# Second attention: heads 0 to 15 of three tiles first, and four projections moved into the steps

## Chip, cores, metric

One core of one Trainium2 chip. The metric is the time of one execution of the whole program on the device, in microseconds, as the median of several runs. Where a part of the program is meant, its time is read from the trace.

## The reference

Four layers run one after the other on a residual stream `x` of 2048 rows and 576 columns: attention (A), gMLP (B), A, B. The change touches the second A alone.

```python
def _A_ref(x, wqkv, wo):            # H = 32 heads of Dh = 18; W = 8 keys at distance 0, 2, .. 14 back
    qkv = (x @ wqkv)...             # q, k, v by head
    logits = einsum('bhsd,bhswd->bhsw', q, kg) * Dh ** -0.5     # masked where the key lies before row 0
    o = einsum('bhsw,bhswd->bhsd', softmax(logits), vg)
    return o... @ wo
x = x + _A_ref(_layernorm(x), A_wqkv, A_wo)
x = x + _B_ref(_layernorm(x), ...)
x = x + _A_ref(_layernorm(x), A_wqkv, A_wo)
x = x + _B_ref(_layernorm(x), ...)
```

## The kernel before

The attention cuts the rows into 19 tiles of 112 queries with a halo of 16 keys. A *step* `s` is one tile and one half of the heads: tile `s // 2`, heads 0 to 15 where `s` is even, 16 to 31 where it is odd. The main loop runs 38 steps. In each, PE makes the next step's logits (`L_mm`), ScalarE their exponentials (`EXP`), and PE multiplies the previous probabilities by v (`PV`); then come other pieces from a table: projections of q and k for later columns (`PG`), of v (`VW`), output projections of finished rows (`WO`), layer norms.

```python
def L_mm(s):
    t, hf = divmod(s, 2)
    L_tiles[s] = [self.H_tile("L_ps") for _ in range(2)]     # two tiles of two PSUM banks, a ring of 2
    ...                                                      # 16 matmuls, reading QK
def PV(s):
    ...                                                      # 16 matmuls into O_ps, then on VectorE:
    nc.vector.reciprocal(...)
    nc.vector.tensor_tensor(out=o_t[:nq, 288 * hf:288 * (hf + 1)]..., op=ALU.mult)
    if hf == 1:                                              # both halves there: transpose by DMA, from SP
        nc.sync.dma_start_transpose(out=oT[:, :, c0:c0 + nq], in_=o_t[:nq, :])
def WO(i, hh):                                               # row tile i of 128 rows: two tiles of oT
    for c in range(5):
        nc.tensor.matmul(pw[:, 0:288], lhsT=oT[:, c, r0:r0 + P], rhs=wo_sb[...], ...)
```

A projection lands in a staging tile. When the last one of a staging tile is there, eight DMA moves carry it, head by head, to the places in QK where the logits read it; they go to the queues of POOL and SP in turn.

```python
for dst, src in moves:
    dma_rr[0] += 1
    self.dma(dst, src, eng=queues[dma_rr[0] % len(queues)])
...
def XO(i):                                                   # residual rows for two row tiles, 576 KB, from SP
    self.dma(xo[:], x_prev[i * P:(i + 2) * P, :]..., eng=nc.sync)
def XST(i): self.dma(self.xres[li][...], tails[i]["x"][:])   # store, from SP
def LN_T(i): self.ln_T(...)                                  # transpose of the normed rows, from SP
```

The table, and the loop:

```python
PG_END = 14
pre, pgs = pgs[:6], pgs[6:]          # 18 projections; six ahead of the loop
for k_, (d, qk, cc) in enumerate(pgs):
    at(1 + k_ if li == 0 else (k_ * PG_END) // len(pgs), PG, d, qk, cc, True)
for i in range(NS):
    t = -(-(i + 1) * P // QT) - 1    # the last tile that row tile i needs
    s = 2 * t + (6 if li == 0 and t < 10 else 5 if t < NT - 5 else 4 if t < NT - 3 else 3)
    at(s - 5, XO, i); at(s, WO, i, 0); at(s + 1, WO, i, 1) ...
at(PG_END + 2, alloc_win2b)          # weights of the next layer, six loads from POOL, steps 16 to 26
...
for s in range(NST):
    if s + 1 < NST:
        L_mm(s + 1)
        EXP(s + 1)
    PV(s)
    for f, a in table.pop(s, []):
        f(*a)
```

SP issues in program order: output transposes, moves, loads, stores and the transposes of the normed rows all stand in one line.

The softmax here doesn't subtract the row's maximum and nothing guards it: scores larger than these inputs give would overflow.

## Time and profile before

| | value |
|---|---|
| time, median of 3 runs | 1190.21 us (1190.11 to 1192.29) |
| profiled span | 1190.8 us |
| start of the second attention (its first projection) | 601.25 us |
| from there to the start of the layer's last PV, called *layer time* below | 115.68 us |
| from there to the end | 473.89 us |

The last three rows add up to the span. The prediction below shows the page and the stretches of the layer.

### The profile page before, as it was taken

To read this page: it belongs to the slowest core of one execution; us is meant where nothing else is said; L and a number is where in the kernel's file an instruction comes from. 1 tells how busy PE (TensorE), PEld (TensorE's weight loads), DVE (VectorE), ACT (ScalarE), POOL (GpSimd) and SP (SyncE) were. 2 spreads that over 40 slices of the span, in tenths; PEclk is the share of its full clock that TensorE was granted. 3 is DMA by queue.
4 is the path that set the end of the run, shared out by engine and by line. 5 is a ranking of instruction groups with operands and counts; after the bars stand their busy time and mean duration, and the time that the engine had idled before them with its cause. 6 is when DMAs were issued, how large, how long until landed. Compare 5 with 4: busy or idle time off the path is not lost.

```text
span 1190.8 us, 20761 instructions
## 1 busy us (share of the span) xinstructions
PE 1180.2 (99%) x8554; PEld 620.6 (52%) x8554; DVE 547.4 (46%) x1206; ACT 376.6 (32%) x593; POOL 281.5 (24%) x383
## 2 busy tenths in 40 slices
PE   8999999999999999999999999999999999999998
PEld 5567544444444444457755775444444444444677
DVE  8688587333233233245556786753233233233311
ACT  5578677210110110202156786760110110111000
POOL 4768685000000000001153877530000000000000
PEclk9999999999999999999999999999999999999999
DMA  8989992000000000049645999900000000000332
GB/s 195 200 163 199 181 224 65 23 4 9 12 12 12 12 1 11 12 139 291 169 98 117 203 227 196 202 14 9 12 12 1 12 12 12 12 1 28 125 105 73
DMA packets 178104, 101.21 MB, mean 85 GB/s; under 512 B 134336, under 2 KB 159360, under 8 KB 178009
## 3 DMA queue, kind: packets, MB, share of 16 engines
q1 hardware_dynamic: 165144, 78.13, 30.6%
q0 software_dynamic: 6512, 16.00, 5.4%
q10 hardware_dynamic: 6352, 5.75, 1.6%
q8 instruction: 67, 1.10, 0.4%
q14 instruction: 29, 0.23, 0.1%
HBM read 42.39 MB, written 16.53 MB: 49 GB/s over the span
## 4 chain that ended last, share of the span: by engine, by line
PE 94%; DMA 3%; POOL 1%; ACT 0%; issue 0%; SPq 0%; DVE 0%; ACTq 0%; DVEq 0%
PE pg L887 42%; PE pz L869 12%; PE po L941 12%; PE pz L791 11%; PE pp L402 5%; PE pw L494 3%; PE O_ps L457 3%; PE pv L379 3%; PE L_ps L437 2%; DMA oT<-o_t 2%; PE pzs L791 1%; DMA QK<-win2a 1%; POOL QK L77 1%; DMA wqk_sb<-in_A_wqkv_dram 1%; ACT P_sb L446 0%
## 5 line engine op out<-in xcount | busy, mean ns | idle before, releaser
L887 PE MATMUL pg<-Wq,Z 128*128 128x512 bf16 x2304 | 502.8, 379 | 0.0
L887 PEld LDWEIGHTS <-Z 128*128 128x128 bf16 x2304 | 225.3, 98 | 272.0
L891 DVE TENSOR_TENSOR g_tmp<-pg,ln_xn 128x512 f32<-128x512 f32 x144 | 99.6, 692 | 429.2 <-PE pg L887 429.2
L881 ACT ACTIVATE z1T<-pz 128x1024 bf16<-128x1024 f32 x72 | 73.7, 1024 | 513.8 <-PE pz L869 513.6
L77 POOL DMA_DIRECT2D wout<-in_B_w_out_dram x4 | 4.3, 1064 | 604.6 <-PE pg L887 604.6
L941 PE MATMUL po<-wout,Z 128*128 128x288 bf16 x1152 | 141.4, 286 | 0.0
L446 ACT ACTIVATE P_sb<-L_ps 128x896 bf16<-128x896 f32 (+1 forms) x152 | 126.7, 887 | 41.2 <-PE L_ps L437 40.6
L869 PE MATMUL pz<-xnT,w 128*128 128x512 bf16 (+1 forms) x640 | 136.0, 380 | 0.0
L941 PEld LDWEIGHTS <-Z 128*128 128x128 bf16 x1152 | 112.7, 98 | 28.8
L791 PEld LDWEIGHTS <-xnT 128*128 128x128 bf16 (+1 forms) x800 | 66.2, 97 | 81.0 <-issue 23.7
L791 PE MATMUL pz<-win2a,xnT 128*128 128x512 bf16 x384 | 104.8, 380 | 0.0
L892 DVE TENSOR_TENSOR Z<-g_tmp,z1T 128x512 bf16<-128x512 f32 x144 | 99.6, 692 | 9.7
L869 PEld LDWEIGHTS <-w 128*128 128x128 bf16 (+1 forms) x640 | 51.1, 97 | 80.0 <-issue 27.1
L402 PE MATMUL pp<-xnT,wqk_sb 128*128 128x512 bf16 x360 | 83.8, 382 | 0.5 <-DMA wqk_sb<-in_A_wqkv_dram 0.5
L805 ACT ACTIVATE zp<-pz 128x1024 bf16<-128x1024 f32 x64 | 65.5, 1024 | 36.6 <-PE pz L791 32.8
L951 DVE TENSOR_TENSOR x_new<-po,xo 128x288 f32<-128x288 f32 (+1 forms) x64 | 28.8, 455 | 87.6 <-PE po L941 83.5
L791 PE MATMUL pz<-win2b,xnT 128*128 128x512 bf16 (+1 forms) x256 | 65.7, 380 | 0.0
L807 DVE CUSTOM_DVE_ANT_0 Z<-zp 128x1536 bf16<-128x1536 bf16 x32 | 56.6, 1769 | 13.1 <-ACT zp L805 13.0
L77 POOL DMA_DIRECT2D QK<-stg x81 | 50.7, 631 | 36.3 <-DVE stg L371 21.0
L379 PE MATMUL pv<-wv_sb,xnT 128*128 128x288 bf16 (+1 forms) x380 | 55.8, 285 | 0.0
L242 POOL TENSOR_SCALAR ln_xn<-x_new,ln_mv,ln_rstd 128x576 bf16<-128x576 f32 x23 | 52.8, 2294 | 2.0
L402 PEld LDWEIGHTS <-wqk_sb 128*128 128x128 bf16 x360 | 33.2, 98 | 37.2 <-DMA wqk_sb<-in_A_wqkv_dram 1.0
(114 smaller groups left out, 916.9 us busy)
## 6 DMA issues: line engine op xcount, KB each, us to landing
xres<-x_new SPq DMA_DIRECT2D x48, 288.0 KB
xo<-xres SPq DMA_DIRECT2D x32, 288.0 KB
wout<-in_B_w_out_dram POOLq DMA_DIRECT2D x4, 1296.0 KB, 8.5
xo<-xres SPq DMA_DIRECT2D x8, 576.0 KB
w<-in_B_w_in_dram SPq DMA_DIRECT2D x16, 256.0 KB
QK<-stg POOLq DMA_DIRECT2D x53, 72.0 KB, 4.4
QK<-stg SPq DMA_DIRECT2D x41, 72.0 KB
xo<-in_A_x_dram SPq DMA_DIRECT2D x8, 288.0 KB
```

The lines of the kernel that those rows point to most:

```text
L77: return eng.dma_start(out=out, in_=in_)
L379: nc.tensor.matmul(pv[:nk, 0:288], lhsT=self.xnT[:, c, QT * t:QT * t + nk], rhs=wv_sb[:, c, hh * 288:(hh + 1) * 288], start=(c == 0), stop ...
L402: nc.tensor.matmul(pp[:, :], lhsT=w, rhs=self.xnT[:, c, PADL + cc * 512:PADL + (cc + 1) * 512], start=(c == 0), stop=(c == 4))
L446: nc.scalar.activation(out=P_bufs[(2 * s + jp) % 4][:nk, :, :, 0:nq], in_=Lv[:nk, :, :, 0:nq], func=ACT.Exp, scale=scale)
L791: nc.tensor.matmul(pzvs[ci][:, sub * 512:sub * 512 + w], lhsT=self.xnT[r0:r1, c, PADL + i * P:PADL + (i + 1) * P], rhs=win2(c)[r0:r1, c0 + ...
L805: nc.scalar.activation(out=zp[:, c0:c0 + cn], in_=pzvs[ci][:, 0:cn], func=ACT.Gelu_apprx_tanh, accum_out=sums[:, ci:ci + 1])
L869: nc.tensor.matmul(pz1s[q // 2][:, q % 2, :], lhsT=w1[r0:r1, c, sub * P:(sub + 1) * P], rhs=self.xnT[r0:r1, c, PADL + q * 512:PADL + (q + ...
L881: nc.scalar.activation(out=z1T[:, q2 * 512:(q2 + 2) * 512], in_=pz1s[q2 // 2][:, :, :].rearrange("p a b -> p (a b)"), func=ACT.Gelu_apprx_ ...
L887: nc.tensor.matmul(pg[:, :], lhsT=Z[:, jj, i, sub * P:(sub + 1) * P], rhs=Wq[q][:, i, :], start=(i == 0), stop=(i == NS - 1))
L891: nc.vector.tensor_tensor(out=tmp[:], in0=pg[:, :], in1=bsp[:, qs], op=ALU.add)
L892: nc.vector.tensor_tensor(out=uT(jj)[:, sub, qs], in0=tmp[:], in1=z1Ts[jj, sub][:, qs], op=ALU.mult)
L941: nc.tensor.matmul(acc[hh], lhsT=uT(j // 2)[:, j % 2, i * P:(i + 1) * P], rhs=wouts[j // NJH][:, j % NJH, hh * 288:(hh + 1) * 288], start= ...
```

## The change

Heads 0 to 15 need only the projections that come first, so three tiles of them can go ahead while the moves for heads 16 to 31 still land. That lets the loop begin after two projections rather than six, and the other four run within the steps, beside the exponentials.

```diff
         NST = 2 * NT
+        seq = list(range(NST))
+        if li > 0:
+            seq[0:6] = 0, 2, 4, 1, 3, 5
+        pbi = {s: 2 * k_ for k_, s in enumerate(seq)}
@@ EXP and PV: the probability buffers follow the position, not the step
-  P_bufs[(2 * s + jp) % 4]
+  P_bufs[(pbi[s] + jp) % 4]
@@
-        pre, pgs = pgs[:6], pgs[6:]
+        npre = 6 if li == 0 else 2
+        pre, pgs = pgs[:npre], pgs[npre:]
@@ the loop
-                L_mm(s + 1)
-                EXP(s + 1)
-            PV(s)
+                L_mm(seq[s + 1])
+                EXP(seq[s + 1])
+            PV(seq[s])
```

With 16 projections in the table, the rule `(k_ * PG_END) // len(pgs)` puts the last at step 13; with 12 it was step 12.

More of the change, by code (lines that the diff above doesn't have):

```diff
@@ L445, in EXP @@
                 Lv = L_ps[:, :, 0:4 * QT].rearrange("p a (b c) -> p a b c", c=QT)
-                nc.scalar.activation(out=P_bufs[(2 * s + jp) % 4][:nk, :, :, 0:nq], in_=Lv[:nk, :, :, 0:nq], func=ACT.Exp,
+                nc.scalar.activation(out=P_bufs[(pbi[s] + jp) % 4][:nk, :, :, 0:nq], in_=Lv[:nk, :, :, 0:nq], func=ACT.Exp,
                                      scale=scale)
@@ L457, in PV @@
                         nc.tensor.matmul(O_ps[:, idx * (DH + 1):(idx + 1) * (DH + 1)],
-                                         lhsT=P_bufs[(2 * s + jp) % 4][:nk, jj, ftl, :],
+                                         lhsT=P_bufs[(pbi[s] + jp) % 4][:nk, jj, ftl, :],
                                          rhs=v_ext[:nk, t, 16 * hf + idx, :], start=True, stop=True)
@@ L698, in layer_A @@
             if k_ == (2 if li == 0 else 0):
-                L_mm(0)
-                EXP(0)
+                L_mm(seq[0])
+                EXP(seq[0])
             PG(d, qk, cc, li > 0 or k_ < 4, q2)
```

## The prediction

> **What bounds the kernel now.** I began with the page: busy shares, then the chain of work that ended last.
>
> ```profile
> PE 1180.2 (99%) x8554; PEld 620.6 (52%) x8554; DVE 547.4 (46%) x1206; ACT 376.6 (32%) x593; POOL 281.5 (24%) x383
> ...
> PE 94%; DMA 3%; POOL 1%; ACT 0%; issue 0%; SPq 0%; DVE 0%; ACTq 0%; DVEq 0%
> ```
>
> PE is the bound from one end to the other, so the only thing that a reordering can win is time in which PE waits. The change touches the second attention alone (the branch with `li > 0`). In the ordered chain that layer runs from 601.4 us, where its first projection starts, to about 717.5 us, where the gMLP's first matmuls appear. I cut that into stretches:
>
> ```profile
> core 0: us, PE busy (x) PEld busy (x) DVE busy (x) ACT busy (x) POOL busy (x), PEclk, DMA share, GB/s
> 625.70:632.60 6.90, 6.90 (x49) 3.08 (x50) 3.46 (x5) 2.03 (x3) 3.77 (x8) 1.00 0.32 67
> 632.60:645.00 12.40, 12.40 (x225) 6.91 (x227) 8.44 (x18) 10.35 (x12) 4.70 (x8) 1.00 0.43 94
> 645.00:647.20 2.20, 1.82 (x46) 1.26 (x46) 1.41 (x3) 1.77 (x3) 1.07 (x2) 1.00 1.28 261
> 647.20:666.10 18.90, 18.89 (x279) 12.19 (x282) 12.53 (x31) 12.92 (x19) 10.08 (x14) 1.00 0.80 165
> 683.20:689.40 6.20, 5.71 (x119) 4.04 (x119) 3.96 (x12) 5.68 (x9) 5.55 (x7) 1.00 0.97 249
> ```
>
> Columns are length, then each engine's busy time. The first row is the six projections that stand ahead of step 0: PE full, ACT nearly empty (2.03 of 6.90). The second is steps 0 to 5, the third step 6 into 7, the fourth steps 7 to 12. PE is visibly idle only in the third row (0.38) and the last (0.49). But busy PE hides short waits, because the ends of matmuls are modelled; the chain shows them as lengths of the logits group (L_ps):
>
> ```profile
> 634.57 0.59 PE L_ps L437 x16
> 635.16 0.49 PE O_ps L457 x16
> 635.66 1.09 PE pp L402 x5
> 636.75 0.37 PE L_ps L437 x14
> 637.12 0.49 PE O_ps L457 x16
> 637.61 1.09 PE pp L402 x5
> 638.71 0.60 PE L_ps L437 x16
> ```
>
> The unhindered group takes 0.33 to 0.37 us; every other one takes 0.60. The timeline of ScalarE says why:
>
> ```profile
> 633.02 1.73 ACT L446 ACTIVATE P_sb<-L_ps 128x896 bf16<-128x896 f32 x2 [5.21 <-PE L_ps L437]
> 634.97 1.73 ACT L446 ACTIVATE P_sb<-L_ps 128x896 bf16<-128x896 f32 x2 [0.23 <-PE L_ps L437]
> 637.15 0.92 ACT L446 ACTIVATE P_sb<-L_ps 128x896 bf16<-128x896 f32 x1 [0.46 <-PE L_ps L437]
> ```
>
> The pair of exponentials of a step takes 1.73 us and begins 0.47 us after PE reaches that step's logits (634.50 in the timeline, 634.97 here). The next step's second half of logits needs the two banks that the second exponential frees. So a step that follows an undelayed one must last some 2.2 us, and where PE has less work than that it waits. A delayed step pays the next one's wait: losses come in every second step.
>
> **What the Trainium skill says.** Perfetto Trace Analysis, Identifying the Most-Contended Engine: matmul busy time is not a good measure for PE, since pipelined instructions look smaller in the trace. This trace agrees: 99% busy, with waits of 0.25 us inside. The same page, Optimization Strategy, says that regimes with different most-contended engines can gain by being interleaved. That is the idea here: a PE-only stretch (6.90 us, ACT at 2.03) goes into steps where ACT has little slack. It helps only in steps where PE waits. ScalarE: Activation LUTs, Rules for kernel authors, budgets about 0.3 us per ACTIVATE and 0.83 ns per element, 1.04 us for the 896 elements of one exponential; the trace has 0.87 to 0.92, and I use the trace. DMA: Bandwidth & Descriptors, Anatomy of one DMA, puts the fixed cost of a DMA at about 2 us, mostly the receipt; the trace has a median of 4.4 us from issue to landing for the QK moves from POOL.
>
> **The change, part by part.** Nothing is added or removed: same matmuls, exponentials, evacuations and moves.
>
> (1) *Four projections leave the head of the loop.* A projection is 1.09 us of PE (5 matmuls, chain above), so step 0 comes 4 x 1.09 = 4.4 us sooner and the same 4.4 us return within the steps. Sum on PE: zero.
>
> (2) *Where they return.* Before, 12 projections sit in steps 0-5 and 7-12, one each; step 6 has none. After, 16 lie in steps 0 to 13: step 0 has two, steps 1-6 one, step 7 two, steps 8-13 one. So steps 0, 6, 7 and 13 gain one each. From the chain, the pieces of a step are logits 0.33, PV 0.49, projection 1.09, v projection 0.61, output projection 0.61.
>
> Before, the loss against pure PE work is: steps 1, 3, 5 last 2.18 rather than 1.92, about 0.24 each, together 0.7. Step 6 has only 0.33 + 0.49 + 0.61 = 1.43 of work, and the wait follows (chain, step 6 to 7):
>
> ```profile
> 645.44 0.04 ACT P_sb L446
> 645.48 0.77 issue
> 646.25 0.92 ACT P_sb L446
> 647.16 0.04 issue
> 647.21 0.37 PE L_ps L437 x8
> ```
>
> From 645.03 to 650.39, two steps last 5.36, against 1.43 + 3.14 = 4.57: 0.79 lost. Steps 8 to 12 last 3.14 with 3.13 of work: none.
>
> After: step 0 has 3.00 of work, no loss; the alternation shifts by one, so steps 2, 4, 6 pay some 0.25 each, again 0.7. Step 6 has 2.52 and step 7 4.22, no loss beside that. The stall of 0.79 is gone: **-0.8 us**. The projection in step 0 and the one in step 7 merely fill steps that had no loss.
>
> (3) *Step 13's projection.* Before, steps 14 to 20 last 2.22, 2.06, 2.22, 2.11, 2.18, 2.13, 2.16 = 15.08 against 7 x 2.06 = 14.42. A long step 13 lets ACT catch up, so step 14 should have no loss and the alternation begins at 15: at best 0.16 less, at worst nothing by step 20, where ACT's backlog is again what it was. I take **-0.1**. The stall in 683.2 to 689.4 (steps 21 and 22 have no output projection: 6.21 us for 1.45 + 1.45 + 2.06 = 4.96 of work) stays.
>
> (4) *Heads 0-15 first.* Logits of heads 16-31 read the last moves of the first column half. With two projections ahead, the natural order would ask for them 4.4 us sooner, at about 628.3, when POOL is still issuing them (its issues run from 627.45 to 630.03). The new order asks at position 3: 625.74 + 0.33 + 2.18 + 3.00 + 1.92 = 633.2. Is that late enough?
>
> ```profile
> 625.70:631.00 5.30, 5.30 (x41) 2.50 (x41) 2.48 (x4) 2.03 (x3) 3.77 (x8) 1.00 0.42 87
> 631.00:636.40 5.40, 5.40 (x82) 2.84 (x80) 3.75 (x8) 3.15 (x4) 0.00 (x0) 1.00 0.00 0
> ```
>
> The DMA engines carry nothing after 631.0, so all has landed 2 us ahead. It is a guard for part (1) and costs 0. Sum: 1190.2 - 0.9 = **1189.3 to 1189.4**.
>
> **Rivals.** *A: new wait for moved data.* Position 1 (tile 1, heads 0-15) reads what tile 0 read without a wait. The last second-half moves leave after step 13 rather than 12. They end issuing on SP at 669.8 before and are wanted at 676.8; after, issued about 1.3 later and wanted 0.9 earlier, so the slack of 7.0 becomes 4.8, against landings of 2.6 to 5.5 us. Tight only in the worst case: then up to +0.7, leaving 1190. *B: the attention output.* Tile 0 is transposed by DMA in step 3 rather than 1, and tile 3 writes the same output buffer in step 6, some 5 us later; tile 1 is finished one step nearer to the first output projection, about 8 us ahead of it. The transpose at 636.47 shows its packets by 639. Should transposes queue behind moves on SP, DVE would wait about a microsecond, and four single-bank PSUM buffers cushion PE; +0 to +1. *C: the interleaving gains all that it hides.* If ACT bounded the loop, starting it 4.4 us sooner would end it 4.4 us sooner: 1185.8. Against it: in 647.2 to 666.1 ACT is busy 12.92 of 18.90 and PE all of it, and the PE work that leaves the head comes back in the loop. *D: a clash of evacuations in the double steps.* DVE in step 7 has 2 x 0.69 + 0.26 + 0.46 + 0.45 = 2.6 us in 4.2; no.
>
> **Range and chances.** The three runs span 1190.11 to 1192.29, so a median can lie a microsecond high; A and B can eat the gain; C in part could double it. 1188.5 to 1190.7 holds eight in ten. Two per cent is 24 us, five times the projections moved: within 2% 0.985, faster 0.005, slower 0.01.
>
> **What would show it.** In the profile after, PE's idle time of 0.38 near step 6 to 7 is gone, step 6 lasts about 2.5 to 2.8 us, and the logits groups of 0.6 sit at positions 2, 4, 6. Step 13 lasts 3.15. The stall around step 21 stays at about 1.2 us. The gMLP's first matmuls begin 0.7 to 1.1 us sooner, and all behind them keeps its length. A wait of PE on a QK move or an output transpose would mean A or B; a gain above 2 us would mean that I misread the loop's bound.

## More of the kernel before

SP's own line of issues around steps 12 to 15 (start, length, then the transfer; a start here is the moment of the issue, not the landing):

```profile
666.71 3.11 SPq L77 DMA_DIRECT2D QK<-stg  x4
669.93 1.38 SPq L469 DMA_TRANSPOSE oT<-o_t  x1
671.42 1.21 SPq L249 DMA_TRANSPOSE xnT<-ln_xn  x1
672.68 0.58 SPq L77 DMA_DIRECT2D xres<-x_new  x1
673.36 0.38 SPq L77 DMA_DIRECT2D xo<-xres  x1
673.83 1.21 SPq L469 DMA_TRANSPOSE oT<-o_t  x1
```

There is no gap between these: SP is full. The first row is SP's half of the moves of the last projection (step 12), the second the transpose of tile 6, the last that of tile 7. Row tile 6 needs tile 7, and its output projection stands in step 19.

## The result

| | before | changed |
|---|---|---|
| median | 1190.28 us (4 runs) | 1193.78 us (4 runs: 1191.66, 1192.27, 1195.29, 1195.44) |
| profiled span | 1190.8 | 1193.7 |
| start of the second attention | 601.25 | 600.09 |
| layer time | 115.68 | 119.69 |
| rest | 473.89 | 473.89 |

The ratio is 1.0025, with an interval of 1.0002 to 1.0048: slower by a little, not faster, and far inside 2%.

The layer took 4.0 us longer. The chain of waits of the changed kernel shows where:

```profile
674.32 0.45 PE pw L498 x4
674.77 7.06 DMA oT<-o_t
681.83 0.05 issue
681.88 1.14 PE pw L498 x5
683.02 0.51 PE L_ps L441 x16
683.53 0.53 PE O_ps L461 x16
684.06 1.21 PE pv L379 x5
```

The output projection (pw) at 681.88 waited for a transpose that SP had issued at 674.77, 7.06 us before. The five matmuls of one such piece take 0.61 us elsewhere; here they take 1.14, and those of v 1.21 rather than 0.63. The stretches say why (in each row PE's busy time comes second, after the length; the granted clock stands third from the right):

```profile
676.00:678.60 2.60, 2.60 (x46) 1.79 (x43) 2.31 (x8) 2.29 (x4) 2.21 (x2) 1.00 1.07 275
678.60:681.90 3.30, 0.06 (x2) 0.03 (x2) 0.74 (x3) 0.82 (x2) 3.04 (x3) 1.00 1.11 184
681.90:685.90 4.00, 4.00 (x47) 2.46 (x47) 1.63 (x4) 1.73 (x2) 0.66 (x2) 0.57 1.38 295
```

PE stood still for 3.24 us, and then ran at 0.57 of its clock for 4 us. In the layer's own time, counted from its start, step 19's PV began at 78.03 before and 77.35 after, so the changed kernel was 0.68 ahead; step 22's began at 84.48 and 88.49, so it was 4.01 behind, and it stayed so. The 4.7 us between are 3.24 of waiting and about 1.45 of slow clock.

SP's line shows why the transpose was late:

```profile
666.82 1.24 SPq L473 DMA_TRANSPOSE oT<-o_t  x1
668.15 3.11 SPq L77 DMA_DIRECT2D QK<-stg  x4
671.38 1.23 SPq L249 DMA_TRANSPOSE xnT<-ln_xn  x1
672.65 1.54 SPq L77 DMA_DIRECT2D xres<-x_new  x1
674.30 0.38 SPq L77 DMA_DIRECT2D xo<-xres  x1
674.77 1.21 SPq L473 DMA_TRANSPOSE oT<-o_t  x1
```

The four moves now stand behind tile 6's transpose rather than ahead of it. From the layer's start, tile 6 left at 68.7 before and 66.7 after, but tile 7 at 72.6 before and 74.7 after: 2.1 later, while PE was ready to use it 0.5 sooner, at 78.5 (81.8 less the wait) rather than 79.1. Before, 6.5 us lay between issue and use, and PE did not wait. After, 3.9 did, and the landing took 7.1.

The trace also records the semaphore updates by which a transfer reports that it has landed, 16 for each of these transposes. They tell a landing even where nobody waits for it. In the kernel before, tile 7's transpose landed 5.6 us after its issue, only 0.9 us ahead of its use; in a second profile of it (before_again) it was 5.4 and 1.3. So that kernel was itself within about a microsecond of this wait.

### The profile page after: what moved, and what is told of

Same layout as the page of the kernel before. It is cut to its first block, busy times and chain, and to the rows that moved or that the text cites. A ratio compares the mean times of both kernels' runs of the same rounds, so it can differ in the third digit from the quotient of the medians. Undisturbed runs are those within 1.5% of the kernel's fastest.

```text
span 1193.7 us, 20762 instructions
## 1 busy us (share of the span) xinstructions
PE 1181.4 (99%) x8554; PEld 621.3 (52%) x8554; DVE 548.0 (46%) x1206; ACT 376.7 (32%) x593; POOL 283.3 (24%) x383
## 4 chain that ended last, share of the span: by engine, by line
PE 94%; POOL 2%; DMA 1%; DVE 1%; issue 1%; ACT 1%; SPq 0%; POOLq 0%; ACTq 0%; DVEq 0%
PE pg L892 42%; PE pz L874 12%; PE po L946 12%; PE pz L796 10%; PE pp L402 6%; PE pv L379 3%; PE pw L498 3%; PE O_ps L461 3%; PE L_ps L441 2%; PE pzs L796 1%; DMA xnT<-ln_xn 1%; DMA oT<-o_t 1%; POOL ln_xn L242 1%; ACT P_sb L450 0%; POOL stg L242 0%
## 5 line engine op out<-in xcount | busy, mean ns | idle before, releaser
L498 PE MATMUL pw<-wo_sb,oT 128*128 128x288 bf16 x320 | 49.2, 288 | 3.9 <-DMA oT<-o_t 3.5
```

## The experiments

The theory (Q): the place of the last projection's moves in SP's line delays tile 7's transpose past its use. Rivals: the new order of heads does it (H); the 576 KB loads ahead of it in SP's queue do (R), or POOL's weight loads, which are in flight at the same time (W); the engines are so full that any shift waits somewhere (D); it is one profile's jitter (J). "Layer" is the layer time of the profiled run, "tile 7 leaves" and "used" (in step 19; in step 20 in the two kernels with wo_later's edit) count from the layer's start.

| kernel | median us | before, same rounds | ratio | layer | tile 7 leaves / used | waits of PE for a DMA in the layer |
|---|---|---|---|---|---|---|
| before | 1190.28 | | | 115.68 | 72.6 / 79.1 | none |
| before_again | 1193.46 (1 run) | 1191.31 | | 115.69 | 72.4 / 79.1 | none |
| changed | 1193.78 | 1190.28 | 1.0025 | 119.69 | 74.7 / 81.8 | 3.24 at step 19 |
| again | 1194.35 | 1191.20 | 1.0022 | 117.27 | 74.3 / 79.8 | 1.23 at step 19, 0.79 at step 25 |
| after_third | 1193.46 (1 run) | 1192.60 | | 118.29 | 74.7 / 80.4 | 1.82 at step 19 |
| order_only | 1195.92 | 1191.20 | 1.0035 | 119.41 | 76.1 / 82.8 | 2.09 at step 7 |
| pre2_only | 1198.54 | 1191.20 | 1.0060 | 120.86 | 76.6 / 81.1 | 1.7 at the start, 1.84 at step 25 |
| end12 | 1190.01 | 1191.20 | 0.9986 | 115.13 | 71.8 / 78.6 | none |
| end12_second | 1193.46 | 1192.60 | 1.0005 | 115.15 | 72.1 / 78.4 | none |
| last12 | 1191.17 | 1191.31 | 1.0005 | 115.09 | 72.7 / 78.6 | none |
| last12_second | 1195.90 (1 run) | 1192.60 | | 116.00 | 72.7 / 78.7 | 0.13 at step 19, 0.61 at step 25 |
| last15 | 1194.76 | 1192.60 | 1.0007 | 117.03 | 70.1 / 80.3 | 1.2 at step 18, on QK moves |
| before_last13 | 1191.63 | 1191.31 | 1.0004 | 116.63 | 73.5 / 79.2 | 0.71 at step 25 |
| moves_pool | 1194.78 | 1191.95 | 1.0017 | 115.91 | 70.7 / 79.2 | 0.81 at step 18, on a QK move |
| win2b_late | 1192.77 | 1191.95 | 1.0005 | 115.65 | 74.1 / 78.5 | 0.48 at step 25 |
| xo_pool | 1195.47 | 1191.95 | 1.0032 | 117.61 | 74.5 / 78.7 | 0.17 at step 19, 1.10 at step 25, 0.96 at step 29 |
| wo_later | 1192.98 | 1191.95 | 1.0007 | 116.52 | 73.5 / 79.8 | 1.09 at step 25, 0.48 at step 27 |
| end12_wo_later | 1192.36 | 1191.31 | 1.0001 | 114.82 | 71.9 / 79.9 | none |

All outputs are right. Most differences of totals are no larger than the scatter (the kernel before alone ran from 1189.5 to 1195.7), so the layer column carries the argument.

### again and after_third: does it come each time?

No edit.

> The changed kernel once more, to see whether its wait at step 19 (the output projection of row tile 6 waits 3.2 us for the transpose of attention tile 7, then PE runs at a granted clock of 0.57 for 4 us) is fixed or comes and goes. Its four runs fell in two groups, 1191.7 and 1192.3, 1195.3 and 1195.4. Theory Q (the transpose stands later in SP's queue, behind the moves of the last projection, and so lands close to its use): a wait on the output transposes in steps 13 to 20 in nearly every run, its size between 0 and 4 us; median 1191 to 1195. Rival J (jitter of this one profile): no such wait in the new profile and a median of 1189.5.

> A third look at the changed kernel. Theory Q: again a wait on tile 7's transpose at step 19, layer 116.5 to 120. If it is 115 to 115.5, the wait comes only in some executions.

Rival J falls. In all three profiles PE waits for tile 7's transpose at step 19; these two have, in the list of waits (total, times, longest):

```profile
PE pw L498 <- DMA oT<-o_t: 1.2, 1, 1.2
```
```profile
PE pw L498 <- DMA oT<-o_t: 1.8, 1, 1.8
```

The first line is of again, the second of after_third. The landing took 5.4 us in the first and 5.6 in the second, 7.1 in the profile above: the time of leaving is nearly fixed, the landing is not. The landings of 5.4 and 5.6 are no slower than those of the kernel before (5.4 and 5.6). There the lateness alone makes the wait: against the first profile of the kernel before, the transpose leaves 1.75 and 2.10 us later and is wanted 0.5 sooner; less the 0.9 us to spare that is 1.3 and 1.7, and 1.23 and 1.82 were measured. The longer wait of the first profile has a slower landing on top.

The profile of again has one more wait of this kind, 0.79 us at step 25. The list puts it down to VectorE, but the weight load just before it waits for the transpose of tile 10, whose last semaphore update, at 691.30, comes just ahead of its start at 691.34. The slow clock does not follow every wait. In again it did not come. In after_third it did, as the stretches show (the wait ends at 679.9, in the first row):

```profile
678.00:680.00 2.00, 0.18 (x3) 0.12 (x3) 0.75 (x3) 0.83 (x2) 1.73 (x3) 1.00 1.10 338
680.00:681.20 1.20, 1.20 (x32) 0.82 (x31) 0.46 (x1) 0.15 (x1) 1.20 (x1) 0.99 1.23 321
681.20:684.60 3.40, 3.40 (x46) 2.06 (x43) 1.84 (x5) 1.69 (x3) 0.76 (x2) 0.50 1.51 214
```

### order_only and pre2_only: each half alone

```diff
# order_only
-        npre = 6 if li == 0 else 2
+        npre = 6
# pre2_only
-            seq[0:6] = 0, 2, 4, 1, 3, 5
+            pass
```

> Only the new order of heads; six projections ahead and none moved. Theory Q: the last projection is again at step 12, so SP's queue around step 13 is as before and the wait does not come; time within 0.5 us of before (1190.2). Rival H (the order of heads crowds the transposes of tiles 0 to 2 together and sets SP back): 1192 to 1195 as in the changed kernel, with a wait on an output transpose.

> Only the four projections moved into the steps; heads in their old order. The logits of heads 16 to 31 are asked for at step 0, 4.4 us sooner, while their moves are still landing (to about 631 with the layer's start at 601.4): PE waits some 2.5 us at position 1. Theory Q: the wait at step 19 also comes, since the last projection is at step 13; but with the first wait ahead, PE is later and the wait shrinks by what SP gains. Time 1191 to 1195. Rival H: the transposes keep their old spacing, so no wait at step 19: about 1192 from the first wait alone.

The order alone was expected by Q to cost nothing, and that missed: it is the slowest but one. But its wait is another one, at step 7, as the chain shows:

```profile
643.91 5.67 DMA oT<-o_t
649.58 0.14 issue
649.72 0.77 PE pw L498 x5
650.49 0.33 PE L_ps L441 x16
```

(Chain of waits of order_only, start and length.) The first output projection needs tile 1. With the order changed, tile 1 is finished a step later and its transpose stands behind moves: it leaves at 44.8 rather than 40.8 after the layer's start, and lands 5.8 us after. In the changed kernel steps 0, 6 and 7 carry one projection more each, and the same transpose has 8.5 us and no wait. So H is right of this half alone and not of the whole change: moving the projections hid what the order costs.

The projections alone make the wait that the order was meant to prevent: logits waiting for moves at position 1. In the list of PE's waits in the layer (total, times, longest):

```profile
PE pw L498 <- DMA oT<-o_t: 1.8, 1, 1.8
PE L_ps L441 <- DMA QK<-stg: 1.7, 4, 0.8
```

The loop's first PV begins 2.7 us later than in the changed kernel (30.06 against 27.34 from the layer's start), close to the 2.5 expected. The wait for an output transpose came too, but at step 25 and for another tile, not at 19. So the two halves do need each other.

### end12, last12, last15: where the last projection stands

```diff
# end12: all 16 in steps 0 to 12
-               (k_ * PG_END) // len(pgs)
+               (k_ * (PG_END - 1)) // len(pgs)
# last12: only the very last one moved, from 13 to 12
+               min((k_ * PG_END) // len(pgs), 12)
# last15: only the very last one moved, from 13 to 15
+               15 if k_ == len(pgs) - 1 else (k_ * PG_END) // len(pgs)
```

> The whole change, but the 16 projections in steps 0 to 12 rather than 0 to 13 (three double steps), so that the moves of the last one go to SP ahead of the transpose of tile 6, as before. Theory Q: the transpose of tile 7 leaves SP about 3 us sooner and the wait at step 19 is gone or below 1 us: 1189.3 to 1190.5. Rival W (the transpose is slow because the weight load from POOL's queue shares the DMA engines with it at 678 to 681, wherever the moves stand): still 1192 to 1195.

> The changed kernel with one thing moved: the very last projection runs in step 12 (two there) rather than 13; everything else stays, the loads of win2b too. Theory Q (its moves stand in SP's queue between the transposes of tiles 6 and 7, so that of tile 7 leaves at 74.4 us after the layer's start rather than 72): tile 7's transpose leaves near 72, no wait at step 19, layer 115.0 to 115.8, median below the changed kernel's by 2 to 4 us. Rival D (no single cause; the DMA engines are full and any order of this part waits somewhere): waits of 1 us or more turn up at steps 19 to 26 all the same, layer 116.5 or more.

> The changed kernel with its last projection at step 15 rather than 13, so that its moves come behind the transpose of tile 7 in SP's queue. Theory Q (place in the queue): tile 7's transpose leaves at 70 to 72 us after the layer's start, its use at step 19 does not wait; but the logits of position 19 now ask for the moves before they have landed, a wait of 1 to 3 us on a QK move around 75 to 78; layer 116 to 118. Rival D (any late moves crowd the DMA engines and the transposes wait): a wait on a transpose at steps 19 to 21 remains beside it.

> A second look at the changed kernel with its last projection at step 12. Theory Q: layer 115.0 to 115.3 again, no wait on a transpose in steps 13 to 21. Rival D: 116.5 or more.

> The whole change with its projections ended at step 12, once more, perhaps on another chip, to see whether it beats both kernels: layer 115.1, so 0.6 us below the kernel before; total 0.0 to 1.5 us below it, which the scatter of the first attention may hide.

One projection moved by one step takes the wait at step 19 away: the layer is 115.09 rather than 117.3 to 119.7, and 115.13 and 115.15 with all of them a little earlier. SP's line in end12 has the old order again, moves ahead of both transposes:

```profile
665.72 3.15 SPq L77 DMA_DIRECT2D QK<-stg  x4
668.98 1.22 SPq L473 DMA_TRANSPOSE oT<-o_t  x1
...
672.72 1.22 SPq L473 DMA_TRANSPOSE oT<-o_t  x1
```

Moved the other way, to step 15, the moves stand behind tile 7's transpose. It leaves at 70.1, lands long before its use, and no output projection waits. What waits is the logits, as expected, on the late moves themselves (list of PE's waits in the layer, last15):

```profile
PE L_ps L441 <- DMA QK<-stg: 1.2, 2, 1.0
```

That is theory Q's signature: with the same number of moves and bytes, ahead of both transposes or behind both, tile 7 is in time or 0.13 us late; between them, in all three profiles of the changed kernel, it is 1.2 to 3.2 late. (In pre2_only, before_last13, win2b_late, xo_pool and wo_later the moves stand between them too, and tile 7 is in time or 0.17 late; so the place is not enough by itself.) Rival D is not dead either. The second look at last12 missed its expectation of no wait: in last12_second a transpose was 0.61 us late at step 25, and in last12 the piece at step 19 took 0.79 us rather than 0.61, so tile 7 landed just as it was needed.

### before_last13: the converse

```diff
-            at(... (k_ * PG_END) // len(pgs), ...)
+            at(... 13 if k_ == len(pgs) - 1 else (k_ * PG_END) // len(pgs), ...)
```

> The converse: the kernel before with only its last projection moved from step 12 to step 13; order of heads and six projections ahead as before. Theory Q: the transpose of tile 7 leaves 2 to 3 us later than the kernel before's 72.6 and the wait appears in it: layer 116.5 to 119 against 115.7, median 1 to 3 us above before. If the layer stays at 115.7, the late moves alone do not make the wait.

Half a hit. The layer grows by 0.9 us to 116.63, but tile 7 left only 1.0 later (73.5) and had landed 0.6 us before its use; the wait of 0.71 came at step 25, for tile 10. In the kernel before, PE is later than in the changed one, so the same place costs less there. The late moves alone do not make the wait at step 19.

### moves_pool, win2b_late, xo_pool, wo_later: what else takes it away

```diff
# moves_pool: the last eight moves all from POOL
+               *(((nc.gpsimd,),) if li > 0 and d == 4 else ())
# win2b_late: weight loads at steps 22 to 32 rather than 16 to 26
+        w2s = PG_END + (2 if li == 0 else 8)
# xo_pool: residual loads from POOL
-  eng=nc.sync
+  eng=nc.sync if li == 0 else nc.gpsimd
# wo_later: output projections of row tiles up to 8 one step later
-  (6 if li == 0 and t < 10 else ...
+  (6 if t < 10 else ...
```

> The changed kernel with the eight moves of the last projection (step 13) all on POOL, none on SP. Theory Q: SP is 3.1 us freer between the transposes of tiles 6 and 7, so tile 7's leaves near 71.5 us after the layer's start rather than 74.5 and the wait at step 19 goes: layer 115 to 116, median 1190 to 1191. POOL gets 2.4 us more before a layer norm, which is not urgent. Rivals W and R: the transpose leaves sooner but lands behind the same loads; a wait of 1 us or more stays.

> The changed kernel with the six loads of win2b on POOL's queue moved from steps 16 to 26 to steps 22 to 32, out of the way of the transposes of tiles 6 to 8. From the first PV of the layer's first projection on, before took 115.7 us, the changed kernel 119.7 and 117.3 in its two profiles. Theory Q (transpose leaves late in SP's queue): no better than the changed kernel, a wait of 1 to 4 us on an output transpose around step 19. Rival W (the weight load shares the DMA engines with the transpose and holds it up): the wait at step 19 gone, 115 to 116; the median 1.5 to 3 us below the changed kernel's 1194.

> The changed kernel with the 576 KB residual loads (xo) of this layer issued by POOL rather than SP, so that no transpose stands behind one in SP's queue; the bytes stay. Theory R (in SP's queue the transpose of tile 7 waits for the 576 KB load issued 0.4 us ahead of it: its 256-byte packets began when that load's 2304-byte packets ended, 3 us later): the transposes land in 4 to 5 us, no wait at step 19, layer 115 to 116 us. Rivals Q and W: the wait stays within a microsecond of 1 to 4.

> The changed kernel with each output projection of row tiles up to 8 one step later, two steps' more room (about 2.1 us) between transpose and use. All theories that say the transpose has too little room: the waits at step 19 and 20 shrink by about 2 us, so to 0 to 1.5; layer 115 to 117; median 1190 to 1192. If the time stays at 1194, the room at that place is not the cause. The pieces after step 26 may move together and make a wait there instead.

Each of the four takes the wait for tile 7 away (xo_pool leaves 0.17 us of it), two of them against theory Q. With moves_pool tile 7 leaves at 70.7, as Q has it. With win2b_late it leaves as late as ever, at 74.1, and lands after 4.3 us, just in time for its use at 78.5; with xo_pool after 4.2. In the changed kernel it took 5.4 to 7.1. So the lateness at issue was borne where the landing was a microsecond shorter, and W and R may each hold a part of that landing. In wo_later, where no 576 KB load stands right ahead of it, it landed after 3.3. But their shares are not shown: each is one profile, the changed kernel alone differs by 1.7 us from profile to profile, and in pre2_only, with the 576 KB load right ahead, it landed after 4.4, and in the kernel before it took 5.6 although the weight load's packets began only after it had landed. Packets of the changed kernel's trace fit: the 256-byte packets of tile 7's transpose begin at 677.7 us, when the 2304-byte packets of the 576 KB load issued 0.47 us ahead of it are coming to their end (the last starts at 678.3), and from 678 on the 4608-byte packets of a weight load run beside them.

None of the four is a better kernel. The moves crowd POOL and one comes late for the logits; the weight loads moved to later steps leave a wait of 0.48 at step 25, and the rest of the program grows by 0.6 us (474.47), where a wait of 0.64 us ends as tile 16's transpose lands, 6.8 us after its issue; xo_pool waits at steps 25 and 29, and wo_later at 25 and 27.

### end12_wo_later and before_again

```diff
# end12_wo_later: the edit of end12 and that of wo_later
```

> Candidate for the best version: the whole change, projections ended at step 12, output projections of tiles up to 8 one step later. Room for the transposes grows by 2 us at steps 7 to 20. Theory Q: layer 114.5 to 115.3, no wait on a transpose before step 21, median 1189 to 1191 with less scatter than the kernel before. Rival D: no better than 1191 to 1193, because waits move to steps 23 to 26, as they did in the changed kernel with later output projections.

> The kernel before, one more look, to see how far its second attention scatters: 115.7 in its first profile. Theory Q: no wait on a transpose at step 19 (room of 6.5 us there), layer 115.5 to 116.5; the scatter of the total comes from the first attention, whose code all kernels share. Rival D: 117 or more with a wait on a transpose somewhere in the layer.

The combination has the shortest layer of all, 114.82, which is 0.86 below the kernel before, with no wait for a DMA. Its median, 1192.36, is above the 1189 to 1191 that were expected. The kernel before repeats its layer to 0.01 us (115.69), while its start moves from 601.25 to 602.10. In the profiles of all kernels together that start lies between 598.05 and 605.42, though the first attention, which sets most of it (its last PV starts between 126.8 and 133.9 us), has the same code everywhere. In end12_second, for instance, one wait of 4.8 us for a transpose of normed rows ends at 55 us, in the first attention. So 0.6 to 0.9 us won in the second attention do not show in a total: the ratios are 0.9986 (0.9970 to 1.0002) and 1.0005 (0.9982 to 1.0028) for end12 on two occasions, and 1.0001 (0.9988 to 1.0013) for the combination. A version that beats the kernel before is shown for the layer, not for the program.

## Why the prediction was wrong

The prediction said 1189.4, within 1188.5 to 1190.7; the median was 1193.78.

- **Part (1), the sum on PE is zero: right.** PE's pieces keep their lengths, and the rest of the program stays at 473.89 us.
- **Part (2), the stall at step 6 goes and the alternation shifts: right.** The waits of logits sit at positions 2, 4 and 6 (0.63, 0.61, 0.61 in the chain), and at step 14 the changed kernel is 0.89 us ahead of the kernel before. (2.18 less 1.92 is 0.26 a step and not 0.24; the slip stands on both sides of the sum and cancels.)
- **Part (3), another 0.1 from step 13: not so.** Of that lead 0.68 is left at step 19: 0.21 was lost where 0.1 was to be won. This is the only term of the intended gain that was off. (The layers of end12 and last12 are 0.55 and 0.59 shorter than before, but they have no projection in step 13 and so don't measure this term.)
- **Part (4), the order of heads costs 0: wrong in itself, right in the whole.** It looked at the logits alone. The order also moves the transpose of tile 1, and alone that costs 3.7 us of layer time (order_only, 119.41); with the projections moved too, it has the 8 us of room that rival B gave it (8.5 measured).
- **The step that failed is rival B, "+0 to +1".** It asked of the output transposes only at tiles 0, 1 and 3, at the start of the layer, and took their landing from one at 636.47, where the DMA engines had been empty for 5 us. In steps 17 to 26 (tiles 6 to 10) a landing took from 2.5 us (end12, tile 6) to 7.8 (pre2_only, tile 10), and the kernel before has 6.1 to 7.3 us there from issue to use. Rival A did see that the last moves leave after step 13 and did the sum of their slack, but only for the logits that read them. SP ended issuing them 2.6 us later in the layer's time (71.2 against 68.6) and not 1.3, since tile 6's transpose now went ahead of them; the logits did not wait all the same. Rival A did not ask what stands behind them in SP's line. The cost was 3.24 us of waiting in the first profile, 1.2 and 1.8 in the others, and after the two longer ones a slow clock on top.
- **The range** also took the scatter of the total from three runs. Later rounds of the kernel before reach 1195.7.

What stays open: why the landing differs between 5.4 and 7.1 us in the same kernel, and whether and how much each of the two loads adds to it. And step 25 is a second place of the same kind, for which no experiment was made: seven profiles wait there for tile 10, six of them of kernels in which the wait at step 19 is gone, nearly gone or never came, and in before_again that transpose landed only 0.3 us before its use.

## What to carry to other kernels

When work is moved in a schedule, list every queue that carries something for it, and look at what stands *behind* the moved transfers in a queue that is full, not only at who reads them. A wait that the profile before does not show may be short of happening by a microsecond or less: compare the time from issue to use with the landing in a loaded stretch, not in a quiet one. And where unchanged code scatters by more than the effect, split the span at points that every kernel shares and compare the parts.

## What the Trainium skill lacked or had wrong

- TensorE: Matmul & The Clock Gate, What's actually happening, puts the fall to the half clock after at least one idle window of about 3.4 us. Here single waits of 1.8 us (after_third, pre2_only) and 2.1 us (order_only) were followed by a clock of 0.50 for 3.4 us, and in the first attention one of 0.96 us (win2b_late, before 84.2 us); one of 1.60 us (last15, before 134.3 us) and one of 1.23 us (again) were not. So a wait well under a window can be enough, and no sharp limit shows. The length of the slow stretch agrees with the window.
- DMA: Bandwidth & Descriptors, Anatomy of one DMA, gives about 2 us of fixed cost for a DMA that GpSimd issues, and its Latency and other measured facts has no latency of a transpose under load. Here one output transpose of 112 rows and 640 columns, issued from SP in the second attention, took from 2.5 us (end12, tile 6) to 9.9 us (xo_pool, tile 12) from issue to its last semaphore update.
- The same page, Queues, rings and completion order, says that each DMA engine consumes the descriptors of a ring in order. The runs agree, and the page does not say what that costs: a transpose issued 0.47 us after a 576 KB load in the same queue began its packets 2.9 us after its issue.
